# One tile for the attention's seven PSUM banks, handed out by a walk at build time

## The chip, the cores and the metric

The kernel runs on one core of a Trainium2 chip. Its engines work from queues of their own, in order, and wait for one another by semaphores: TensorE (PE) multiplies into PSUM, a memory of eight banks of 128 x 512 fp32; ScalarE (ACT) and VectorE (DVE) read PSUM; GpSimd (POOL) and the DMA queue of SyncE (SP) do not touch it here. The metric is the device time of one execution in microseconds, as the median of several.

## The reference

For x of 2048 tokens by 512 channels it computes a gated mix of attention and a token-mixing MLP:

```python
g = sigmoid((x * gate_w).sum(-1, keepdims=True))
qkv = (x @ wqkv).reshape(B, S, 3, H, Dh)            # S = 2048, H = 32 heads, Dh = 16
scores = einsum("bhqd,bhkd->bhqk", q, k) * Dh ** -0.5
a = einsum("bhqk,bhkd->bhqd", softmax(scores), v)   # then heads joined, @ wo
u = gelu(einsum("bsd,sf->bdf", layernorm(x), w1) + b1)     # F = 1792
b = einsum("bdf,fs->bds", u, w2) + b2               # back to (B, S, D)
return g * a + (1 - g) * b
```

All is fp32. With 32 heads of 2048 x 2048 scores, 134 million exponentials have to be taken, and an engine takes them 128 rows at a time.

## The kernel before, in words

The program has three stretches. Up to some 278 us it projects x to q, k and v (each fp32 product made of three products of split halves) and runs the first layer of the MLP. From 278 to 1231 us it runs the attention, with the second layer of the MLP woven in. A short end adds the last projection and stores the rows.

The attention has 32 groups (NG: 16 pairs of heads by two halves of the queries) of four phases each (PHASES), 128 phases in all, p = 0 to 127. A phase makes 16 score tiles (NSC), n = 0 to 15, each 128 keys by 512 queries, one matmul (line 1067) into one PSUM bank. A score uses 64 of PE's 128 rows; on the other 64 a product of the second layer, of a late projection or of the output projection runs beside it (line 1076, tile `dn`, which holds the eighth bank for itself). `dense` says how many products a phase has beside its scores: 14 in 96 phases, 12 in 32. The scores after that number have no product beside them; two of these that use different halves of the rows (`head`) run side by side.

Each score tile leaves PSUM in one of three ways:

- EVAC, n = 1, 3, 5, 8, 14, 15: DVE copies it to SBUF (line 1089, into `pe`), and one wide ACT instruction per phase takes the exponential of all six there (line 1102).
- SINGLE, n = 0, 2, 4, 6, 7, 9: ACT takes its exponential straight from PSUM (line 1093, 128 x 512).
- TWO, (10, 11) and (12, 13): two scores in neighbouring banks, one ACT instruction over both (line 1031, `exps`, 128 x 1024).

Then `apply_v` multiplies with v (line 963): 64 matmuls in groups of four that run side by side, adding into one bank, `av`. The pairs of scores are used in two lists: HELD (the copied ones, 3 pairs) are those of the phase before, since their wide exponential comes late; TURNS (5 pairs) are this phase's. DVE then adds `av` to a running sum in SBUF (line 985). In the first phase of a group (ph = 0) there are two such sums in two banks, one that ends the group before and one that begins the new group.

Seven banks serve 16 scores and one or two `av`. Before the change a phase opens two pools, one after the other (`regions`). The first has seven tiles of a bank each, for scores 0 to 6, and again for 7, 8 and 9. The second has two tiles of two banks for the pairs, two of one bank for scores 14 and 15, and `av`. `shares` decides which bank is which from the bank that `av` of the phase before had (`spare`), so that score n + 7 always takes the bank of score n, and `av` that of score 9. A score may be written when the tile that lay in its place has been read.

The order of the work on every engine is the order of the program's text (`manual_schedule`). In phases with 12 products beside, the text issues scores 12, 13, 15, 14 (`in_turn`), else 0 to 15 in order. Work of other kinds is hung between: `amid` before score 14's reader, `later` at the end of a phase on DVE, `calls` at its start. `mark` is a memset of one element on DVE that takes several waits at once so that later instructions wait for one engine alone; `evac_done` and `earlier` serve the same end.

Just ahead of the attention, line 549 on DVE reads the last two banks of layer 1 (`late_u`). Behind it, a pool `ps_end` opens seven tiles `pa` where the scores' banks lay; its first use sums the last `av` (lines 1169 and 1170).

Of the kernel before, what the change touches and what calls it, by code (L numbers as in the profile page):

```python
# [9 lines left out]
F32 = mybir.dt.float32  # L10
# [22 lines left out]
NB = 512  # L33
NQ = S // NB
VC = DH + 1
SCALE = DH**-0.5
# [24 lines left out]
def gated_mix(ctx: ExitStack, tc: tile.TileContext, a_x, a_wqkv, a_wo, b_w1, b_b1, b_w2, b_b2, gate_w, out):  # L61
    nc = tc.nc
# [115 lines left out]
    with tc.tile_pool(name="vp", bufs=1, side="right") as pool:  # L178
# [138 lines left out]
        e = pool.tile([P, NS], F32, name="e")  # L317
# [4 lines left out]
        y, t, w = (pool.tile([P, NS], F32, name=n) for n in "ytw")  # L322
# [103 lines left out]
    with tc.tile_pool(name="gl", bufs=2, side="right") as gl:  # L426
# [74 lines left out]
        for f0, cs in order.items():  # L501
            n = min(NB, F - f0) // P
# [32 lines left out]
    ptp = att_ctx.enter_context(tc.tile_pool(name="pt", bufs=2, reuse_waits="tile"))  # L535
# [45 lines left out]
    PHASES, NSC, BANKS = 4, 16, 7  # L581
    LAST = NG * PHASES - 1
# [257 lines left out]
    dense = {}  # L840
# [74 lines left out]

    token, mark = (out_pool.tile([1, 1], F32, name=name, bufs=1) for name in ("token", "mark"))

    EVAC = 1, 3, 5, 8, 14, 15
    SINGLE = 0, 2, 4, 6, 7, 9
    TWO = (10, 11), (12, 13)  # L920
    TURNS = [(0, 2), (4, 6), (7, 9), *TWO]
    HELD = [(1, 3), (5, 8), (14, 15)]

    def shares(n):

        for one in range(0, BANKS, 2):
            lows = [k for k in range(one)][::2] + [k for k in range(one + 1, BANKS)][::2]
            for third in lows:
                if n in (third, third + 1):
                    first, second = (low for low in lows if low != third)  # L930
                    return [first, first + 1, one, second, second + 1, 2 * third + 1 - n, n]


    def regions():
        return tc.tile_pool(name="ps_s", bufs=1, space=PSUM, reuse_waits="tile")

    sums, latest, evac_done = {}, {}, []

# [49 lines left out]

    engines = {getattr(mybir.EngineType, name) for name in ("PE", "Activation", "DVE", "Pool", "SP")}
    with tc.manual_schedule(engines=engines):  # L990
        held, fence, turn, spare = [], None, 0, 0
        landed.clear()

        for p in range(LAST + 1):
# [18 lines left out]
            if n_b == NSC - 2:  # L1013
                head[-2:] = second, 1 - second
            else:
                head[-4:] = second, 1 - second, 1 - second, second
            in_turn = list(range(n_b)) + ([14, 15] if n_b == NSC - 2 else [12, 13, 15, 14])
            qbs = {}
            for a, b in TURNS + HELD:
                if head[a] == head[b]:  # L1020
# [3 lines left out]
                    qbs[zero], qbs[one] = turn, 1 - turn  # L1024
                    turn = 1 - turn

            def exps(n):
                pt = ptp.tile([P, 2, NB], F32, name="p2", bufs=len(TWO))
                where = [share[(j - BANKS) % BANKS] for j in (n - 1, n)]
                low = min(where)  # L1030
                pairs_done.append(nc.scalar.activation(pt, twos[low, low + 1], AF.Exp, scale=SCALE))  # L1031
                for j, k in zip((n - 1, n), where):
                    units[j] = *units[j][:3], pt[:, k - low, :]

            pairs_done = []
            evac = evp.tile([P, len(EVAC), NB], F32, name="pe")
            units = {}
            share = shares(spare)
            pool = regions()
            psum = pool.__enter__()  # L1040
            ones = [psum.tile([P, NB], F32, name=f"s{n}") for n in range(BANKS)]
            for n in in_turn:
                i, qb = head[n], qbs[n]
                c = at[i][qb]
                at[i][qb] += 1
                if n < TWO[0][0]:
                    if n >= BANKS:
                        ones[share[n - BANKS]] = psum.tile([P, NB], F32, name=f"s{share[n - BANKS]}")
                    s = ones[share[n % BANKS]]
                else:  # L1050
                    if n == TWO[0][0]:
                        pool.__exit__(None, None, None)
                        pool = regions()
                        psum = pool.__enter__()
                        twos = {}
                        for low in range(BANKS):
                            if low == share[2]:
                                av = psum.tile([P, NB], F32, name="av")
                            elif low in (share[0], share[1]):
                                twos[low] = psum.tile([P, NB], F32, name=f"u{low}")  # L1060
                            elif low not in twos:
                                two = psum.tile([P, 2, NB], F32, name=f"t{low}")
                                twos[low], twos[low + 1] = two[:, 0, :], two[:, 1, :]
                                twos[low, low + 1] = two
                    s = twos[share[(n - BANKS) % BANKS]]
                rows_i = slice(i * HALF, i * HALF + ROWS)
                nc.tensor.matmul(  # L1067
                    s,
                    kt[grp][rows_i, c * P : (c + 1) * P],
                    qt[grp][rows_i, qb * NB : (qb + 1) * NB],  # L1070
                    start=True,
                    stop=True,
                )
# [8 lines left out]
                if n == in_turn[-2]:  # L1082
                    if n_b and second and beside[-1][-1] in between:
                        between[beside[-1][-1]]()
                    for what, *args in amid.get(p, ()):
                        what(*args)
                if n in EVAC:
                    pt = evac[:, EVAC.index(n), :]
                    nc.vector.tensor_copy(pt, s)  # L1089
                    units[n] = i, c, qb, pt  # L1090
                elif n in SINGLE:
                    pt = ptp.tile([P, NB], F32, name="p1", bufs=len(SINGLE))
                    one = nc.scalar.activation(pt, s, AF.Exp, scale=SCALE)  # L1093
                    if n == SINGLE[-1] and p:
                        tc.add_manual_dep(one.ins, earlier.ins.name, SYNC, reason=EARLY)
                    units[n] = i, c, qb, pt
                else:
                    units[n] = i, c, qb, None
                    if n in (TWO[0][1], TWO[1][1]):
                        exps(n)  # L1100
            for x in ([evac] if p < LAST else [evac[:, :2, :], evac[:, 2:, :]]):
                done = nc.scalar.activation(x, x, AF.Exp, scale=SCALE)  # L1102
# [19 lines left out]
            spare = share[2]  # L1122
# [19 lines left out]
            pool.__exit__(None, None, None)  # L1142
# [168 lines left out]
```

## Time and profile before

| | |
|---|---|
| median of 3 runs | 1265.29 us (1265.22 to 1266.12) |
| the profiled execution: span, first to last instruction | 1263.6 us |
| mean granted clock of PE in it | 0.998 |
| PE busy | 1255.3 us, 99% |
| ACT busy | 1069.0 us, 85% |
| DVE busy | 851.3 us, 67% |
| ACT busy between 500 and 700 us | 200.00 us |
| scores (line 1067), instructions | 2048 |
| exponentials from PSUM, single and pairs | 768 and 256 |

No time of its own was taken of the profiled execution but the span, which is 1.7 us below the median of the runs. How to read it: a row of the timeline is start, duration (us), engine, line, operation, tiles written <- tiles read, shapes, how many were merged, and in brackets the idle time before it with the one who ended it. PE's weight loads have a row of their own (PEld); a matmul that has to wait, waits in its weight load. A row whose instruction starts before the one ahead has ended means that the engine took it into its queue; its duration then holds waiting too. The span of a run of instructions in the timeline is from the first's start to the last's end.

### The profile page before, as it was taken

How to read it: one execution, taken by the hardware profiler on the slowest of the kernel's cores; microseconds unless marked ns; L12 is line 12 of the kernel's file. 1: busy time of each engine (PE TensorE's matmuls, PEld its weight loads, DVE VectorE, ACT ScalarE, POOL GpSimd, SP SyncE). 2: the span in 40 equal slices, each digit the busy share in tenths (PEclk: the TensorE clock that was granted, in tenths of full speed). 3: DMA queues.
4: the chain of work that ended last, by engine and by line, in shares of the span. 5: the costliest groups of instructions: out<-in, count | busy, mean ns of one | idle time of the engine just before them, and what ended most of it. 6: DMA issues, size and time to landing. Idle time of an engine off the chain costs nothing.

```text
span 1263.6 us, 32707 instructions
## 1 busy us (share of the span) xinstructions
PE 1255.3 (99%) x13342; PEld 828.5 (66%) x13342; DVE 851.3 (67%) x1562; ACT 1069.0 (85%) x1405; POOL 198.9 (16%) x316
## 2 busy tenths in 40 slices
PE   9999999999999999999999999999999999999997
PEld 7888888875666666666666666666666666666666
DVE  5675453178767676767677677776777677678883
ACT  4443343269999999999999999999999999999990
POOL 0220444461010101010101101111111111000000
PEclk9999999999999999999999999999999999999999
DMA  4799443243744444544344443443543442366611
GB/s 132 252 333 334 145 120 105 83 129 108 214 122 104 89 102 85 157 86 97 77 105 93 97 93 84 91 88 79 114 102 71 91 100 60 56 164 177 152 59 70
DMA packets 100555, 152.31 MB, mean 121 GB/s; under 512 B 17109, under 2 KB 56171, under 8 KB 96300
## 3 DMA queue, kind: packets, MB, share of 16 engines
q1 hardware_dynamic: 99820, 149.08, 45.9%
q8 instruction: 107, 1.75, 0.6%
q10 hardware_dynamic: 576, 1.05, 0.2%
q14 instruction: 52, 0.43, 0.1%
HBM read 105.39 MB, written 44.68 MB: 119 GB/s over the span
## 4 chain that ended last, share of the span: by engine, by line
PE 99%; ACT 1%; DVE 0%; issue 0%
PE av L963 31%; PE s L1067 22%; PE acc L424 12%; PE t L1067 9%; PE acc L75 8%; PE t L963 5%; PE dn L1076 4%; PE u L1067 3%; PE pa L1162 2%; PE acc L199 1%; PE acc L268 1%; PE acc L245 0%; ACT p L1093 0%; ACT pe L1102 0%; PE dn L1162 0%; PE pa L1192 0%
## 5 line engine op out<-in xcount | busy, mean ns | idle before, releaser
L1093 ACT ACTIVATE p<-s 128x512 f32<-128x512 f32 x768 | 412.4, 791 | 0.1
L1102 ACT ACTIVATE pe<-pe 128x3072 f32<-128x3072 f32 x129 | 381.7, 2961 | 0.0
L1067 PE MATMUL s<-qs,ks 64*128 64x512 f32 x1280 | 330.2, 400 | 0.6 <-ACT p L1093 0.6
L1089 DVE COPY pe<-s 128x512 f32<-128x512 f32 x512 | 318.2, 683 | 4.8 <-PE s L1067 1.1
L1067 PEld LDWEIGHTS s<-qs,ks 64*128 64x128 f32 x1280 | 225.6, 184 | 93.3 <-issue 45.3
L1031 ACT ACTIVATE p<-t 128x1024 f32<-128x1024 f32 x256 | 278.5, 1265 | 0.0
L963 PE MATMUL av<-p,v 128*32 128x256 f32 x3880 | 227.1, 379 | 0.0
L1089 DVE COPY pe<-u 128x512 f32<-128x512 f32 x256 | 164.9, 686 | 72.0 <-PE u L1067 72.0
L963 PE MATMUL av<-pe,v 128*32 128x256 f32 x3072 | 192.5, 383 | 0.0
L985 DVE TENSOR_TENSOR ot<-av,ot 128x512 f32<-128x512 f32 (+2 forms) x160 | 93.2, 583 | 142.3 <-PE av L963 141.0
L68 POOL TENSOR_TENSOR w_lo<-w_raw,w_hi 128x512 fp32r<-128x512 f32 (+1 forms) x128 | 153.1, 1203 | 197.3 <-ACT w_hi L67 100.3
L1076 PE MATMUL dn<-u_hi,w_hi 64*128 64x512 f32 x448 | 181.1, 404 | 0.0
L963 PEld LDWEIGHTS av<-p,v 128*32 128x32 f32 x3880 | 126.0, 110 | 83.3 <-ACT p L1093 0.2
L1076 PE MATMUL dn<-u_hi,w_lo 64*128 64x512 f32 x448 | 180.6, 403 | 0.0
L1076 PE MATMUL dn<-u_lo,w_hi 64*128 64x512 f32 x448 | 180.4, 403 | 0.0
L1067 PE MATMUL t<-qs,ks 64*128 64x512 f32 x512 | 142.2, 412 | 0.0
L963 PEld LDWEIGHTS av<-pe,v 128*32 128x32 f32 x3072 | 86.7, 109 | 82.1 <-ACT p L1093 37.8
L1080 POOL MEMSET token<- 1x1 f32 x128 | 11.4, 89 | 742.2 <-PE dn L1076 701.7
L67 ACT CAST w_hi<-w_raw 128x512 fp32r<-128x512 f32 (+1 forms) x67 | 38.0, 569 | 82.9 <-PE acc L424 63.1
L1067 PEld LDWEIGHTS t<-qs,ks 64*128 64x128 f32 x512 | 72.9, 184 | 51.0 <-ACT p L1093 49.5
L424 PE MATMUL acc<-h_hi,w_hi 128*128 128x512 f32 x224 | 87.9, 392 | 0.0
L424 PE MATMUL acc<-h_hi,w_lo 128*128 128x512 f32 x224 | 87.8, 392 | 0.0
(171 smaller groups left out, 1616.0 us busy)
## 6 DMA issues: line engine op xcount, KB each, us to landing
w_raw<-in_B_w_dram SPq DMA_DIRECT2D x96, 256.0 KB
ks<-kp SPq DMA_DIRECT2D x192, 128.0 KB
qs<-qp SPq DMA_DIRECT2D x256, 64.0 KB
kp<-pc SPq DMA_DIRECT2D x16, 512.0 KB
qp<-pc SPq DMA_DIRECT2D x8, 768.0 KB
qp<-row SPq DMA_DIRECT2D x24, 256.0 KB
v<-v SPq DMA_DIRECT2D x4, 1088.0 KB
x<-in_A_x_dram SPq DMA_DIRECT2D x16, 256.0 KB
```

The costliest lines, as they stand in the source:

```text
L67: copy(hi, src)
L68: return sub(lo, src, hi.bitcast(F32), ALU.subtract)
L75: nc.tensor.matmul(ps, a, b, start=start and n == 0, stop=stop and n == last)
L424: nc.tensor.matmul(p, a, b, start=first and k == 0, stop=last and k == 2)
L963: mm = nc.tensor.matmul(av[32 * j : 32 * (j + 1), i * QC : (i + 1) * QC], vb[b][:, v_at : v_at + 32], pt[:, h * QC : (h + 1) * QC], start= ...
L985: latest["add"] = nc.vector.tensor_tensor(x, y, x, ALU.add)
L1031: pairs_done.append(nc.scalar.activation(pt, twos[low, low + 1], AF.Exp, scale=SCALE))
L1067: nc.tensor.matmul(s, kt[grp][rows_i, c * P : (c + 1) * P], qt[grp][rows_i, qb * NB : (qb + 1) * NB], start=True, stop=True,)
L1076: mm = nc.tensor.matmul(ps, a[half], b[half], start=begin and not second, stop=last and bool(second))
L1089: nc.vector.tensor_copy(pt, s)
L1093: one = nc.scalar.activation(pt, s, AF.Exp, scale=SCALE)
L1102: done = nc.scalar.activation(x, x, AF.Exp, scale=SCALE)
```

## The change

The seven banks become one tile that lives through the whole attention, and each score's bank is a slice of it. Which slice is settled at build time by a new function, `given_out`. It walks through the 128 phases with times that are written in it as constants (a score every 0.2305 us, a single exponential every 0.488 us, a pair 0.914, a copy 0.6 and so on), keeps for each bank when it will be free, and gives each score the bank that is free first; a pair gets the two neighbouring banks of which the later is free first; `av` gets the bank that is free first too. It returns, for each phase, the banks of the 16 scores and of the one or two `av`. `shares`, `regions` and the pools of each phase go. EVAC, SINGLE, TWO, TURNS and HELD are now worked out from a string, KINDS, and all scores are issued in the order 0 to 15.

```diff
-    EVAC = 1, 3, 5, 8, 14, 15
-    SINGLE = 0, 2, 4, 6, 7, 9
-    TWO = (10, 11), (12, 13)
-    TURNS = [(0, 2), (4, 6), (7, 9), *TWO]
-    HELD = [(1, 3), (5, 8), (14, 15)]
-    def shares(n):
...
-    def regions():
-        return tc.tile_pool(name="ps_s", bufs=1, space=PSUM, reuse_waits="tile")
+    KINDS = "sesesessesaabbee"
+    SINGLES = 6
...
+    def given_out():
+        free, vector, scalar, stream, load, wide = [0.0] * BANKS, 0.0, 0.0, 0.0, 0.0, 0.0
+        given = []
+        def first_free(spread=1, at=None):
+            ways = [b for b in range(BANKS + 1 - spread)] if at is None else [at]
+            best = min(ways, key=lambda b: (max(free[b : b + spread]), b))
+            when = max(free[best : best + spread])
+            free[best : best + spread] = [1e9] * spread
+            return best, when
+        for p in range(LAST + 1):
+            singles = len(dense.get(p // 2, ()))
+            bank, open_two, scored, readers = {}, {}, {}, {}
+            copied = []
+            for n, kind in enumerate(KINDS):
+                alone = n < singles or (n - singles) % 2 == 0
+                if kind in "es":
+                    bank[n], when = first_free()
+                elif kind not in open_two:
+                    bank[n], when = first_free(2)
+                    open_two[kind] = bank[n] + 1, when
+                else:
+                    bank[n], when = open_two[kind]
+                start = max(when + 0.05, stream, load) if alone else max(when + 0.05, begun)
+                load = 0.0
+                begun, stream = start, start + 0.2305
+                scored[n] = start + 0.44
+                if kind == "e":
+                    vector = max(vector + 0.6, scored[n] + 0.69)
+                    free[bank[n]] = vector
+                    copied.append(vector)
+                elif kind == "s":
+                    scalar = max(scalar + 0.488, scored[n] + 0.6)
+                    free[bank[n]] = readers[n] = scalar
+                elif kind in readers:
+                    scalar = max(scalar + 0.914, scored[n] + 1.02)
+                    free[bank[n] - 1 : bank[n] + 1] = [scalar] * 2
+                    readers[n] = scalar
+                else:
+                    readers[kind] = None
+            done = sorted([x for x in readers.values() if x] + [readers[two[1]] for two in TWO])
+            scalar = max(scalar, max(copied) + 0.25) + 0.4267 * len(EVAC) + 0.093
+            sums = [first_free()]
...
+            vector = max(vector + 1.6, at + 1.0)
+            free[sums[-1][0]] = vector
+            load = at + 0.3
+            given.append(([bank[n] for n in range(NSC)], [b for b, _ in sums]))
+        return given
...
-        held, fence, turn, spare = [], None, 0, 0
+        held, fence, turn = [], None, 0
+        given = given_out()
+        scores_ctx = ExitStack()
+        ps_s = scores_ctx.enter_context(tc.tile_pool(name="ps_s", bufs=1, space=PSUM, reuse_waits="tile"))
+        banks = ps_s.tile([P, BANKS, NB], F32, name="banks")
...
-            head = [second if n < n_b else (second + NSC - 1 - n) % 2 for n in range(NSC)]
...
-            in_turn = list(range(n_b)) + ([14, 15] if n_b == NSC - 2 else [12, 13, 15, 14])
+            head = [second if n < n_b else (second + n - n_b) % 2 for n in range(NSC)]
...
+            bank, av_banks = given[p]
...
+                pairs_done.append(nc.scalar.activation(pt, banks[:, low : low + 2], AF.Exp, scale=SCALE))
...
-            share = shares(spare)
-            pool = regions()
-            psum = pool.__enter__()
-            ones = [psum.tile([P, NB], F32, name=f"s{n}") for n in range(BANKS)]
-            for n in in_turn:
+            av = banks[:, av_banks[0]]
+            for n in range(NSC):
...
-                    s = twos[share[(n - BANKS) % BANKS]]
+                s = banks[:, bank[n]]
...
-            tc.add_manual_dep(done.ins, pairs_done[0].ins.name, SYNC, reason=EARLY)
+            tc.add_manual_dep(done.ins, pairs_done[-2].ins.name, SYNC, reason=EARLY)
             evac_done.append(done)
-            earlier = pairs_done[1]
+            earlier = pairs_done[-1]
...
-                    spare = share[3]
-                    av = twos[spare]
+                    av = banks[:, av_banks[1]]
...
-            pool.__exit__(None, None, None)
...
+        scores_ctx.close()
```

More of the change, by code (lines that the diff above doesn't have):

```diff
@@ L916, in gated_mix @@
     token, mark = (out_pool.tile([1, 1], F32, name=name, bufs=1) for name in ("token", "mark"))
-    EVAC = 1, 3, 5, 8, 14, 15
-    SINGLE = 0, 2, 4, 6, 7, 9
-    TWO = (10, 11), (12, 13)
-    TURNS = [(0, 2), (4, 6), (7, 9), *TWO]
-    HELD = [(1, 3), (5, 8), (14, 15)]
-    def shares(n):
[L926 to L931, printed above, removed]
@@ L934, in regions @@
-    def regions():
-        return tc.tile_pool(name="ps_s", bufs=1, space=PSUM, reuse_waits="tile")
+    KINDS = "sesesessesaabbee"
+    SINGLES = 6
+    EVAC = [n for n, kind in enumerate(KINDS) if kind == "e"]
+    SINGLE = [n for n, kind in enumerate(KINDS) if kind == "s"]
+    TWO = [tuple(n for n, kind in enumerate(KINDS) if kind == two) for two in sorted(set(KINDS) - {"e", "s"})]
+    assert all(len(two) == 2 for two in TWO) and len(KINDS) == NSC
+    own = sorted([(n, n) for n in SINGLE] + [(two[1], n) for two in TWO for n in two])
@@ new lines, in gated_mix @@
+    own = [n for _, n in own]
+    kept = list(EVAC)
+    if len(own) % 2:
+        own.remove(SINGLE[-1])
+        kept.append(SINGLE[-1])
+    TURNS, HELD = ([(x[i], x[i + 1]) for i in range(0, len(x), 2)] for x in (own, kept))
+    def given_out():
[40 more added lines that the diff above has]
+            sums = [first_free()]
+            at = max(stream + 0.12, sums[0][1])
+            at += 0.2157 * 2 * len(HELD)
+            if p % PHASES == 0 and p:
+                free[sums[0][0]] = at + 1.1
+                sums.append(first_free())
+                at = max(at, sums[1][1])
+            for i in range(0, 2 * (len(done) // 2), 2):
+                at = max(at, done[i + 1] + 0.05) + 0.2157 * 2
+            vector = max(vector + 1.6, at + 1.0)
[3 more added lines that the diff above has]
+        return given
@@ L1025, in gated_mix, with exps @@
                     turn = 1 - turn
-            def exps(n):
+            bank, av_banks = given[p]
+            def exps(two):
                 pt = ptp.tile([P, 2, NB], F32, name="p2", bufs=len(TWO))
[L1029 to L1033, printed above, removed]
+                low = bank[two[0]]
+                assert bank[two[1]] == low + 1
+                pairs_done.append(nc.scalar.activation(pt, banks[:, low : low + 2], AF.Exp, scale=SCALE))
+                for k, j in enumerate(two):
+                    units[j] = *units[j][:3], pt[:, k, :]
             pairs_done = []
@@ L1045, in gated_mix @@
                 at[i][qb] += 1
[L1046 to L1051, printed above, removed]
-                        pool.__exit__(None, None, None)
[L1053 to L1064, printed above, removed]
-                    s = twos[share[(n - BANKS) % BANKS]]
+                s = banks[:, bank[n]]
                 rows_i = slice(i * HALF, i * HALF + ROWS)
@@ L1081, in gated_mix @@
                         tc.add_manual_dep(fence.ins, mm.ins.name, SYNC, reason=REASON)
-                if n == in_turn[-2]:
+                if n == NSC - 2:
                     if n_b and second and beside[-1][-1] in between:
@@ L1091, in gated_mix @@
                 elif n in SINGLE:
-                    pt = ptp.tile([P, NB], F32, name="p1", bufs=len(SINGLE))
+                    pt = ptp.tile([P, NB], F32, name="p1", bufs=SINGLES)
                     one = nc.scalar.activation(pt, s, AF.Exp, scale=SCALE)
@@ L1098, in gated_mix @@
                     units[n] = i, c, qb, None
-                    if n in (TWO[0][1], TWO[1][1]):
-                        exps(n)
+                    for two in TWO:
+                        if n == two[1]:
+                            exps(two)
             for x in ([evac] if p < LAST else [evac[:, :2, :], evac[:, 2:, :]]):
                 done = nc.scalar.activation(x, x, AF.Exp, scale=SCALE)
-            tc.add_manual_dep(done.ins, pairs_done[0].ins.name, SYNC, reason=EARLY)
+            tc.add_manual_dep(done.ins, pairs_done[-2].ins.name, SYNC, reason=EARLY)
             evac_done.append(done)
-            earlier = pairs_done[1]
+            earlier = pairs_done[-1]
             if n_b and second and beside[-1][-1]:
@@ L1121, in gated_mix @@
             turns, now_held = ([tuple(units[n] for n in pair) for pair in pairs] for pairs in (TURNS, HELD))
-            spare = share[2]
             if ph == 0:
@@ L1141, in gated_mix @@
                 last_ot = ot
-            pool.__exit__(None, None, None)
             held = now_held
```

4 lines of the change are left out of this document (removed).

## The prediction, made before the result was known

> **What bounds the kernel now.** The page first: which engines are full, and where the chain of work runs.
>
> ```profile
> span 1263.6 us, 32707 instructions
> ...
> PE 1255.3 (99%) x13342; PEld 828.5 (66%) x13342; DVE 851.3 (67%) x1562; ACT 1069.0 (85%) x1405; POOL 198.9 (16%) x316
> ...
> PE 99%; ACT 1%; DVE 0%; issue 0%
> ```
>
> The chain lies on PE to 99%, but that alone does not make PE the limit: a busy PE may be one that is held back. So next the window of the attention, which is all that the change touches.
>
> ```profile
> core 0: us, PE busy (x) PEld busy (x) DVE busy (x) ACT busy (x) POOL busy (x), PEclk, DMA share, GB/s
> 286.00:1227.00 941.00, 940.37 (x11838) 577.00 (x11840) 685.22 (x1285) 941.00 (x1146) 98.88 (x220) 1.00 0.45 104
> ```
>
> Here ACT is busy for 941.00 of 941.00 us and PE for 940.37, at a granted clock of 1.00. Two engines are full, so the question is which one paces. The timeline of ACT around the middle shows one phase (16 score tiles), and the timeline of the same phase shows who waits.
>
> ```profile
> 699.47 3.00 ACT L1102 ACTIVATE pe<-pe 128x3072 f32<-128x3072 f32 x1
> ...
> 702.16 3.24 ACT L1093 ACTIVATE p<-s 128x512 f32<-128x512 f32 x6
> 705.05 2.19 ACT L1031 ACTIVATE p<-t 128x1024 f32<-128x1024 f32 x2
> 706.88 3.01 ACT L1102 ACTIVATE pe<-pe 128x3072 f32<-128x3072 f32 x1
> 709.58 0.80 ACT L1093 ACTIVATE p<-s 128x512 f32<-128x512 f32 x1
> ```
> ```profile
> 701.63 0.49 PE L1067 MATMUL s<-qs,ks 64*128 64x512 f32 x1
> ...
> 702.39 2.48 DVE L1089 COPY pe<-s 128x512 f32<-128x512 f32 x4
> 702.39 0.69 DVE L1089 COPY pe<-s 128x512 f32<-128x512 f32 x1
> ...
> 703.81 0.39 PE L1067 MATMUL s<-qs,ks 64*128 64x512 f32 x1
> ...
> 703.99 0.18 PEld L1067 LDWEIGHTS t<-qs,ks 64*128 64x128 f32 x1 [0.22 <-ACT p L1093]
> ...
> 704.03 0.46 PE L1067 MATMUL t<-qs,ks 64*128 64x512 f32 x1
> ...
> 704.48 0.18 PEld L1067 LDWEIGHTS t<-qs,ks 64*128 64x128 f32 x1 [0.19 <-ACT p L1093]
> ...
> 704.97 0.19 PEld L1067 LDWEIGHTS u<-qs,ks 64*128 64x128 f32 x2 [0.19 <-ACT p L1093]
> ...
> 705.46 1.02 PEld L963 LDWEIGHTS av<-pe,v 128*32 128x32 f32 x24 [0.30 <-ACT p L1093]
> 705.46 1.50 PE L963 MATMUL av<-pe,v 128*32 128x256 f32 x24
> ...
> 706.78 2.34 PE L963 MATMUL av<-p,v 128*32 128x256 f32 x40
> ...
> 709.05 0.18 PEld L1067 LDWEIGHTS s<-qs,ks 64*128 64x128 f32 x1 [0.41 <-issue]
> 709.05 0.50 PE L1067 MATMUL s<-qs,ks 64*128 64x512 f32 x1
> ```
>
> From the start of score 0 (call it T = 701.63) to the next one at 709.05 is 7.42 us. Within it PE waits for ACT four times in these rows: for a bank that an exp has still to read. That is the sign that ACT paces and PE follows. How closely it follows is told by a phase in which PE ran without such waits, and by three wide exps after a short starvation of ACT.
>
> ```profile
> 1124.73 0.50 PE L1067 MATMUL s<-qs,ks 64*128 64x512 f32 x1
> ...
> 1132.05 0.49 PE L1067 MATMUL s<-qs,ks 64*128 64x512 f32 x1
> ```
> ```profile
> 343.40 3.00 ACT L1102 ACTIVATE pe<-pe 128x3072 f32<-128x3072 f32 x1
> ...
> 348.98 2.19 ACT L1031 ACTIVATE p<-t 128x1024 f32<-128x1024 f32 x2
> 351.10 2.77 ACT L1102 ACTIVATE pe<-pe 128x3072 f32<-128x3072 f32 x1
> ...
> 358.44 2.83 ACT L1102 ACTIVATE pe<-pe 128x3072 f32<-128x3072 f32 x1
> ```
>
> PE alone needs 1132.05 - 1124.73 = 7.32 us a phase. ACT needs 7.42: the wide exps start 7.70 and 7.34 apart (343.40, 351.10, 358.44), but end, by start plus duration, at 346.40, 353.87 and 361.27, 7.47 and 7.40 apart. A start 0.28 late cost the end some 0.05. So ACT has a queue that hides lateness, and its ends keep 7.42 whatever its starts do. PE has only 7.42 - 7.32 = 0.10 us to spare in each of 128 phases. That is the number on which this prediction turns.
>
> How long is ACT's queue? An exp that starts behind a full queue takes 0.80 (the row at 709.58); the one behind the starved wide exp took 581 ns:
>
> ```profile
> L1093 ACT ACTIVATE p<-s 128x512 f32<-128x512 f32 x1 | 0.6, 581 | 0.0
> ```
>
> The difference, 0.22, is how late score 0 can come without ACT standing still. The wide exp gives a like number: it began 351.10 - 348.98 = 2.12 after the pairs where it usually begins 706.88 - 705.05 = 1.83 after them, 0.29 late, and lost 0.05, so 0.24. I take 0.20 as the lag of PE that ACT forgives, since both readings are upper ends for a phase in which both points are late; 0.15 and 0.30 are kept for the range.
>
> **The change part by part.** No matmul, exp, copy or transfer is added or removed; SP's and POOL's queues get the same instructions in the same order. KINDS spells the same six copied, six single and four paired scores, and TURNS and HELD come out as the same lists. The last wide exp is tied to pairs_done[-2] and the next phase to pairs_done[-1]; with two pairs these are the old [0] and [1]. In the 32 phases with 12 products beside, the issue order 12, 13, 15, 14 becomes 12, 13, 14, 15, but the halves of the rows still alternate, so the same two scores run side by side and two copies on DVE change places. All that costs 0.
>
> What changes is which bank a score gets, and so for which reader PE waits. Write e4 for the exp of score 4, c5 for the copy of score 5. Relative to T, a weight load that waited for e4 began at 703.99, 2.36; for e6 at 704.48, 2.85; for for e7 at 704.97, 3.34; for e9 (av) at 705.46, 3.83. Four copies take 2.48 from 702.39, the first alone 0.69, so they end 0.60 apart; with 0.05 to wake PE they free banks at 1.50 (c1), 2.09 (c3), 2.69 (c5) and 3.29 (c8). A score that waited ends 0.50 after its weight load; those that run freely end 0.23 apart; score 0 ends at 0.50. Score 14 would freely end at 0.50 + 14 x 0.23 = 3.73, and the next T follows 3.59 after it: 7.32, as measured. To keep ACT's 7.42, score 14 may end at 3.83.
>
> Old: every phase reuses banks in one order: scores 7 to 15 take those freed by e0 c1 e2 c3 e4 c5 e6 e7 c8, which is the order of their release (c8 and e7 aside, and those two scores run together). No other order can be quicker. Score 10 also waits for the second bank of its pair, e4, so it ends at 2.36 + 0.50 = 2.86 instead of 2.80; this wait goes with the shared tile, and is worth nothing, since score 11 needs e4 at the same time and ACT is full anyway.
>
> New: I followed given_out() line by line for its bank numbers alone (its times are not used). After the first four phases 27 different orders occur in 124 phases, because a pair needs two neighbouring banks and takes the pair whose later bank comes first. Phase 18, for one, gives scores 0 to 6 banks 3 4 5 6 1 2 0, 7 to 9 banks 3 4 5, the pairs 1 2 and 3 4, and 14, 15 banks 6 0. So score 12 waits for e7 and 13 for c8. It ends score 12 at 3.84, 13 at 4.07, 14 at 4.30, 0.47 over 3.83. If PE already lags ACT by 0.20, everything that ACT frees comes 0.20 earlier on PE's clock, what DVE frees does not: 12 at 3.64, 13 at 3.87, 14 at 4.10, 0.27 over. Since PE can lag by no more than 0.20 without starving ACT, that 0.27 is lost.
>
> The same sum for all 124 phases, carrying the lag from one phase to the next (a phase in the old order gives back 0.10 at most, 0.04 at a lag of 0.20, where c8 holds score 15), comes out thus; after each class what a phase is over at a lag of 0 and of 0.20:
> - 38 phases in the old order or one as good: 0.01 and -0.04; lost 0.05 in all
> - 13 with c3 and e6 for 12 and 13 (e6 then holds 13): 0.06 and 0.06; lost 0.2
> - 26 with e6 for score 10 or 11: 0.22 and 0.02; lost 0.4
> - 26 with e7 for 13: 0.24 and 0.04 to 0.06; lost 1.2
> - 5 with c8 for 13: 0.19 and 0.19; lost 0.7
> - 16 with e7 for 12, or e6 for 10 ahead of c5 and c3: up to 0.48 and 0.29; lost 3.8
>
> Sum 6.3 us. With 0.10, 0.15, 0.25, 0.30 and 0.50 for the forgiven lag the same sum gives 13.0, 9.6, 4.2, 3.4 and 1.8.
>
> Six phases of before already start their wide exp late, as at 351.10; the last is this:
>
> ```profile
> 1209.66 2.19 ACT L1031 ACTIVATE p<-t 128x1024 f32<-128x1024 f32 x2
> 1211.80 2.77 ACT L1102 ACTIVATE pe<-pe 128x3072 f32<-128x3072 f32 x1
> ```
>
> There DVE's extra work has used up the queue, so PE's lag of 0.20 is lost once in each: 6 x 0.2 = 1.2.
>
> **The start.** Here the two views are DVE against PE as layer 1 ends.
>
> ```profile
> 277.44 1.40 DVE L549 TENSOR_SCALAR row<-acc,b 128x512 f32<-128x512 f32 x2
> ...
> 277.77 0.50 PE L1067 MATMUL s<-qs,ks 64*128 64x512 f32 x1
> ...
> 278.23 0.18 PEld L1067 LDWEIGHTS s<-qs,ks 64*128 64x128 f32 x1 [0.28 <-DVE row L549]
> ...
> 278.30 1.30 ACT L1093 ACTIVATE p<-s 128x512 f32<-128x512 f32 x2
> ```
>
> L549 reads the last two banks of layer 1 until 277.44 + 1.40 = 278.84. The old first phase leaves late banks to late scores (banks 1 and 0 go to scores 5 and 6), and score 1 alone waits, for the first of the two reads. The new one gives score 0 bank 0, and one tile over seven banks is first written when all are free. So score 0 moves from 277.77 to 278.84 + 0.05 = 278.89. Old, the wait of score 1 left a hole in ACT: two exps take 1.30 from 278.30 where 0.58 + 0.48 would do (six take 705.05 - 702.16 = 2.89). That hole of 0.2 closes: 1.1 - 0.2 = 0.9, with 0 (waits per bank that find bank 0 free) and 1.1 as ends.
>
> **The end.** The end's seven tiles open where the one tile lay, and must await both last additions rather than one.
>
> ```profile
> 1231.02 0.76 DVE L985 TENSOR_TENSOR ot<-av,ot 128x256 f32<-128x256 f32 x2 [0.48 <-PE av L963]
> ...
> 1231.68 0.59 PE L1169 MATMUL pa<-ot,sums_of 128*128 128x256 f32 x2
> ```
>
> They end at 1231.02 + 0.76 = 1231.78; with 0.05 the matmul moves from 1231.68 to 1231.83, +0.1 (0 to 0.15). PE also leaves the attention with its lag of 0.2.
>
> **Sum.** 0.9 + 6.3 + 1.2 + 0.1 + 0.2 = 8.7 us. The profiled span is 1263.6, 1.7 under the median of 1265.29; span 1272.3, so 1274.0 in the runs' terms.
>
> **Rivals.**
> (a) No measurable change, the other side: ACT forgives far more than 0.20. The place is the wide exp, 2.7 us of work in one instruction; decided at a lag of about 0.5, where the sum is 1.8 and the six phases cost nothing. 1265.3 + 0.9 + 1.8 = 1268, or 1266 to 1267 if the start is free as well. Against it: 0.29 already cost 0.05.
> (b) Faster: 7.42 is not ACT's but a loop over PE (e9 frees av, av ends, score 0, exp 0; exp 0 starts 0.03 after 709.05 + 0.50), and a freer PE brings 7.32: 127 x 0.10 = 12.7, so 1253. Against it: ends 7.40 apart where starts were 7.34.
> (c) A bigger loss: ACT forgives 0.10 to 0.15 only, as DVE's copies of 14 and 15 shift with PE. 9.6 to 13.0 and 2.4 beside: 1277 to 1281.
> (d) The guard is on the tile, not the bank, and scores wait for readers of other banks. A score every 0.50 + 0.48 instead of 0.23 adds some 0.75 x 16 x 128 = 1500 us. The code before had pair tiles of two banks whose waits were for both, which is a small case of it. The Trainium skill, "PSUM — Partial Sum Buffer", section "PSUM bank collisions raise a hardware error", asks that PSUM be guarded by bank and quadrant, by bank in the simple version, not by address: by that rule a bank is enough and (d) is not needed; no run here shows it yet.
> (e) The clock: PE's more frequent short waits lower the granted clock. At half speed a phase of PE takes 7.32 more; in one phase of twenty that is 6 x 7.32 = 44 us, 1318. The row at 286.00 has 1.00 although PE waits up to 0.41 at a time. The Trainium skill, "TensorE: Matmul & The Clock Gate", section "A second HAM failure mode: psum-queue depth-cycling", tells of a kernel whose short idles between groups of matmuls, from cycling through PSUM banks, made the clock swing between half and full; the trace so far does not agree.
>
> **How the numbers follow.** Forecast 0.64, with its own range 1270 to 1279 (lags 0.15 to 0.30, start 0 to 1.1); (a) 0.12, (b) 0.04, (c) 0.16, (d) 0.02, (e) 0.02. About 0.2%, 2.5 us, is what can be told from no change here. Slower is the forecast, (c), (d) and (e): 0.84; same (a): 0.12; faster (b): 0.04. The range reaches into (a), to 1266, and over (c), to 1286; it leaves out (b), (d), (e) and an edge of (a) and (c).
>
> **What would show it.** Right: idle of ACT before L1093 or L1102 in the window 286 to 1227, some 6 to 8 us in all where there was none; phases of 7.42 mixed with some of 7.6 to 7.8; weight loads of scores 11 to 13 waiting for ACT or DVE by 0.2 to 0.5; score 0 at 278.9. Wrong: wide exps ending 7.42 apart throughout, or score 0 at 277.8.

## The result: three times the time

The changed kernel takes 3986.49 us (3982.20 to 3987.83, 4 runs) against 1265.36 us (1265.22 to 1266.12) for the kernel before on the same chip: a ratio of 3.150 [3.146, 3.155]. The forecast was 1274.0. The profiled span is 3983.9 us. The page of the changed kernel, the lines that answer to those of before (PEclk is the granted clock of PE in 40 slices of the span, in tenths):

```profile
span 3983.9 us, 32292 instructions
...
PE 2437.3 (61%) x13342; PEld 1088.5 (27%) x13342; DVE 906.6 (23%) x1562; ACT 1193.0 (30%) x1405; POOL 197.8 (5%) x316
...
PEclk9996565656656565666656556665555655556667
...
PE 63%; ACT 18%; DVE 16%; issue 3%; DVEq 0%
...
L1099 PE MATMUL banks<-qs,ks 64*128 64x512 f32 x2048 | 1393.2, 714 | 1408.1 <-ACT p L1125 524.4
L1099 PEld LDWEIGHTS banks<-qs,ks 64*128 64x128 f32 x2048 | 515.7, 269 | 2288.3 <-ACT p L1125 870.2
...
L1016 PE MATMUL banks<-p,v 128*32 128x256 f32 x5120 | 402.4, 474 | 32.0 <-DVE ot L1038 31.2
L1016 PE MATMUL banks<-pe,v 128*32 128x256 f32 x3072 | 355.6, 632 | 99.5 <-DVE mark L1144 50.9
```

The counts of instructions are those of before (PE 13342, ACT 1405, DVE 1562). No engine is full any more, and the chain runs through all three in turn. That is how work looks that is handed from one engine to the next, one piece at a time. The timeline shows the hand:

```profile
2000.22 0.60 ACT L1125 ACTIVATE p<-banks 128x512 f32<-128x512 f32 x1 [2.46 <-PE dn L1108]
...
2000.87 0.79 PE L1099 MATMUL banks<-qs,ks 64*128 64x512 f32 x1 [0.68 <-ACT p L1125]
...
2001.69 0.60 ACT L1125 ACTIVATE p<-banks 128x512 f32<-128x512 f32 x1 [0.88 <-PE dn L1108]
...
2002.35 0.79 PE L1099 MATMUL banks<-qs,ks 64*128 64x512 f32 x1 [0.69 <-ACT p L1125]
...
2003.17 0.69 DVE L1121 COPY pe<-banks 128x512 f32<-128x512 f32 x1 [3.84 <-PE dn L1108]
...
2003.92 0.79 PE L1099 MATMUL banks<-qs,ks 64*128 64x512 f32 x1 [0.78 <-DVE pe L1121]
```

One score, its reader, the next score: 1.48 us a step after an exp, 1.57 after a copy, where before the scores went 0.23 apart. With seven banks to write to, each score waits until the score just ahead of it has been read. The view of waits counts it:

```profile
PEld banks L1099 <- ACT p L1125: 870.2, 768, 1.2
PEld banks L1099 <- DVE pe L1121: 789.6, 640, 1.3
...
PEld banks L1099 <- ACT p L1085: 462.4, 256, 1.8
...
PEld banks L1099 <- DVE ot L1038: 164.7, 127, 1.5
```

The columns are us in total, times, longest. 768 + 640 + 256 + 127 = 1791 waits, which is 14 in each of 128 phases, less the first: behind every single exp, five of six copies, every pair, and the addition of `av`. Only the second score of each pair does not wait. The four sum to 2286.9 of the 2288.3 us that the scores' weight loads stood idle.

The books close on PE. Before, a phase was 3.83 us of scores (701.63 to 705.46) and 3.59 of multiplying with v (705.46 to 709.05): 490 and 460 us over 128 phases. After, the scores have 1393.2 us of matmuls and 1408.1 of idle ahead of them, the products with v 402.4 + 355.6 and 32.0 + 99.5. That is 3690.8 - 950 = 2741 us more, against 3983.9 - 1263.6 = 2720 in the spans. The 950 are one phase times 128, so the last 21 us are not accounted for.

### The profile page after: what moved, and what is told of

Read it like the earlier page. It is cut to its first block, busy times and chain, and to the rows that moved or that the text cites. A ratio compares the mean times of both kernels' runs of the same rounds, so it can differ in the third digit from the quotient of the medians.

```text
span 3983.9 us, 32292 instructions
## 1 busy us (share of the span) xinstructions
PE 2437.3 (61%) x13342; PEld 1088.5 (27%) x13342; DVE 906.6 (23%) x1562; ACT 1193.0 (30%) x1405; POOL 197.8 (5%) x316
## 4 chain that ended last, share of the span: by engine, by line
PE 63%; ACT 18%; DVE 16%; issue 3%; DVEq 0%
PE banks L1099 35%; PE banks L1016 19%; DVE pe L1121 13%; ACT p L1125 12%; ACT p L1085 7%; PE acc L424 4%; PE acc L75 3%; DVE ot L1038 2%; PE dn L1108 1%; PE pa L1193 1%; PE acc L199 0%; PE acc L268 0%; DVEq L1038 0%; PE acc L245 0%; DVE mark L1144 0%
## 5 line engine op out<-in xcount | busy, mean ns | idle before, releaser
L1099 PE MATMUL banks<-qs,ks 64*128 64x512 f32 x2048 | 1393.2, 714 | 1408.1 <-ACT p L1125 524.4
L1099 PEld LDWEIGHTS banks<-qs,ks 64*128 64x128 f32 x2048 | 515.7, 269 | 2288.3 <-ACT p L1125 870.2
L1121 DVE COPY pe<-banks 128x512 f32<-128x512 f32 x768 | 531.1, 692 | 2245.2 <-PE dn L1108 1263.0
L1125 ACT ACTIVATE p<-banks 128x512 f32<-128x512 f32 x768 | 458.6, 597 | 1856.2 <-PE dn L1108 1331.3
L1016 PE MATMUL banks<-p,v 128*32 128x256 f32 x5120 | 402.4, 474 | 32.0 <-DVE ot L1038 31.2
L1016 PE MATMUL banks<-pe,v 128*32 128x256 f32 x3072 | 355.6, 632 | 99.5 <-DVE mark L1144 50.9
L1085 ACT ACTIVATE p<-banks 128x1024 f32<-128x1024 f32 x256 | 262.1, 1024 | 321.7 <-PE banks L1099 175.1
L1108 PE MATMUL dn<-u_lo,w_hi 64*128 64x512 f32 x448 | 316.5, 706 | 0.0
L1108 PE MATMUL dn<-u_hi,w_hi 64*128 64x512 f32 x448 | 313.6, 700 | 0.0
L1016 PEld LDWEIGHTS banks<-p,v 128*32 128x32 f32 x5120 | 198.0, 141 | 259.3 <-issue 143.2
L424 PE MATMUL acc<-h_hi,w_hi 128*128 128x512 f32 x224 | 87.9, 392 | 0.0
L424 PE MATMUL acc<-h_hi,w_lo 128*128 128x512 f32 x224 | 87.8, 392 | 0.0
```

What stands on the lines that cost most here:

```text
L424: nc.tensor.matmul(p, a, b, start=first and k == 0, stop=last and k == 2)
L1016: mm = nc.tensor.matmul(av[32 * j : 32 * (j + 1), i * QC : (i + 1) * QC], vb[b][:, v_at : v_at + 32], pt[:, h * QC : (h + 1) * QC], start= ...
L1085: pairs_done.append(nc.scalar.activation(pt, banks[:, low : low + 2], AF.Exp, scale=SCALE))
L1099: nc.tensor.matmul(s, kt[grp][rows_i, c * P : (c + 1) * P], qt[grp][rows_i, qb * NB : (qb + 1) * NB], start=True, stop=True,)
```

## The experiments

Four theories were set against each other. **G**: the program's guard, the waits that keep a bank from being written before it is read, follows the tile, whatever bank a score takes. **W**: the walk's order of banks costs the time. **K**: the clock does. **O**, which came up on the way: the order costs more than the prediction's sum. Kernel 4, say, is the kernel of experiment 4.

**1. The old order in the one tile.** given_out() returns the numbers that `shares` gave; all else is as changed.

```diff
     def given_out():
+        def shares(n):
...
         for p in range(LAST + 1):
+            share = shares(spare)
+            bank = [share[n % BANKS] for n in range(NSC)]
+            bank[12:14] = sorted(bank[12:14])
+            sums = [share[2]] + ([share[3]] if p and p % PHASES == 0 else [])
+            spare = sums[-1]
```

> The changed kernel with the bank numbers of the kernel before (score n + 7 takes the bank of score n), in the one tile. Theory G (the waits are set per tile, so that a score waits for the reader of the score before it, in whatever bank): as slow as the changed kernel, 3900 to 4050 us. Rival W (the order in which the walk hands out banks is what costs): back near 1265 us. Rival K (the clock falls of itself because of short waits of PE, and the order brings those waits): near 1265 us too, at a granted clock near 1.00.

Measured in one run: 3984.49 us, as the changed kernel. W and K expected some 1265. So the walk's order is not what costs the 2720 us; the loss comes with the one tile.

**2. The walk's order in the old pools.** The kernel before, with the bank numbers and the order of issue of the change.

```diff
+            bank, av_banks = given[p]
...
-            share = shares(spare)
...
-                    s = twos[share[(n - BANKS) % BANKS]]
+                    s = twos[bank[n]]
```

> The kernel before with its two pools per phase and its separate tiles, but with the bank numbers and the issue order of the walk. Theory G: about the blind forecast, since only the order is left: 1274 us, 1268 to 1280, at a granted clock near 1.00; PE waits 0.2 to 0.5 us ahead of scores 11 to 13 in many phases. Rival W: near 3986 us. If PE's lag is forgiven by ACT to any depth: 1266 us.

Measured: 1303.44 us (1303.12 to 1303.71), ratio 1.0300 [1.0286, 1.0314]. W's 3986 is out, but G's own figure of 1274 is missed too: the order costs 38 us in these pools where the prediction's sum gave 9. That opened O, to which experiments 8 and 9 return.

**3 and 4. PE's waits by bank, in the one tile.** Each score, and the first product of each `av`, waits for the last readers of its own bank alone, with the walk's order (3) and the old one (4). The readers' own waits are left as they were.

```diff
+    def wrote(mm, b, *source):
+        mine = readers.get(b, [])
...
+        tc.declare_no_dep(mm.ins, group="bank readers", keep=keep, reason="other banks")
+        for x in mine:
+            tc.add_manual_dep(mm.ins, x.ins.name, SYNC, reason="this bank was read")
...
+                wrote(sc, bank[n])
```

> The changed kernel (one tile, banks by the walk), but each score and each sum told to wait for the readers of its own bank alone: the waits for other banks are taken off, those for the own bank stated by hand. Theory G: 1274 us as for the walk in old pools, at most 2 us off, since the work and the banks are the same and the pair's first score no longer waits for the second bank. Rival W: near 3986 us.

> One tile with the bank numbers of the kernel before, and waits per bank. Theory G: 1265 to 1267 us, the kernel before but for the start (up to 1.1 us, if the first score waits for all seven banks). Rival that a tile of seven banks costs something of itself (long patterns, other semaphores): above 1270.

Measured: 2011.53 us, ratio 1.590 [1.588, 1.592], and 2017.20, 1.594 [1.592, 1.596]. Half a cure, which no theory had foreseen: G's figures are missed by some 740 and 750 us. The waits and the timeline of kernel 4 name the rest:

```profile
DVE pe L1113 <- ACT p L1117: 440.6, 507, 2.6
ACT p L1117 <- DVE pe L1113: 361.6, 441, 1.1
DVE pe L1113 <- ACT p L1072: 319.4, 128, 2.8
```
```profile
1009.73 0.60 ACT L1117 ACTIVATE p<-banks 128x512 f32<-128x512 f32 x1 [0.82 <-DVE pe L1113]
1010.36 0.69 DVE L1113 COPY pe<-banks 128x512 f32<-128x512 f32 x1 [0.72 <-ACT p L1117]
...
1011.15 0.60 ACT L1117 ACTIVATE p<-banks 128x512 f32<-128x512 f32 x1 [0.82 <-DVE pe L1113]
```

ACT and DVE take turns: an exp waits for the copy of another bank, the copy for the exp. Exp to exp is 1.42 us: 0.60 + 0.69, and 0.13 for two wake-ups. So the guard on the tile also sets its two readers one behind the other. Why it does so, when both only read, no run here shows.

**5 and 6. All waits by bank, in the one tile.** As 3 and 4, and ACT's and DVE's readers no longer wait for each other.

```diff
+    def has_read(inst, *of, own="ACT"):
+        tc.declare_no_dep(inst.ins, group="DVE" if own == "ACT" else "ACT", reason="other banks")
+        tc.add_to_no_dep_group(own, inst.ins)
...
+                    has_read(one, bank[n])
```

> One tile, banks by the walk, with waits per bank for PE and now also none left between a copy on DVE and an exp on ACT of different banks (the run with PE's waits alone set per bank stayed at 2011 us, and its trace showed the readers waiting for each other). Theory G, with the order's cost as the blind sum has it: 1274 us, 1268 to 1280. Rival O (the order alone costs more than the sum, as the 1303 us of the walk in old pools say): 1285 to 1303. If the guard has yet another part: far above 1303.

> One tile, bank numbers of the kernel before, waits per bank for all three engines. Theory G: 1265 to 1267 us, since then nothing is left of the change but the first score's wait for all seven banks (0.9 us). Rival that a tile of seven banks costs something of itself: above 1270.

Measured: walk 1269.27 us (1269.11 to 1269.86), ratio 1.0031 [1.0019, 1.0042]; old order 1265.55 (1265.06 to 1266.12), 1.0002 [0.9993, 1.0011]. Both lie in G's ranges. With the waits by bank the one tile costs nothing that the time shows, and the walk some 4 us. The other 2717 us (3986.49 - 1269.27) go with the waits for banks that an instruction does not touch; the fall of the clock (experiment 7), which goes with them too, is in that sum.

Where the 4 us lie is told by the last matmul of layer 1 (L424) and the first and the 127th wide exp, in the kernel before, in 5 and in 6:

```profile
277.45 0.39 PE L424 MATMUL acc<-h_hi,w_lo 128*128 128x512 f32 x1
...
283.21 2.83 ACT L1102 ACTIVATE pe<-pe 128x3072 f32<-128x3072 f32 x1
...
1219.14 2.83 ACT L1102 ACTIVATE pe<-pe 128x3072 f32<-128x3072 f32 x1
```
```profile
277.26 0.39 PE L424 MATMUL acc<-h_hi,w_lo 128*128 128x512 f32 x1
...
283.92 2.84 ACT L1173 ACTIVATE pe<-pe 128x3072 f32<-128x3072 f32 x1
...
1223.15 2.77 ACT L1173 ACTIVATE pe<-pe 128x3072 f32<-128x3072 f32 x1
```
```profile
277.01 0.39 PE L424 MATMUL acc<-h_hi,w_lo 128*128 128x512 f32 x1
...
283.67 2.84 ACT L1134 ACTIVATE pe<-pe 128x3072 f32<-128x3072 f32 x1
...
1219.42 2.85 ACT L1134 ACTIVATE pe<-pe 128x3072 f32<-128x3072 f32 x1
```

By start plus duration the ends of the wide exps are 935.93 apart before, 939.16 in 5 and 935.76 in 6. The walk costs 3.2 us in 126 phases. Layer 1 ends a few tenths apart in the three traces, so the start is counted from its last matmul: the first wide exp ends 8.59 us after it starts before, and 9.50 in 5 and in 6. The start costs 0.91 in both, though the time of 6 does not show it.

**7. The clock alone.** In the changed kernel the tile has six banks, and on the seventh PE repeats each score's matmul three times, so that its pauses are filled. The result uses none of these.

```diff
-    PHASES, NSC, BANKS = 4, 16, 7
+    PHASES, NSC, BANKS = 4, 16, 6
...
+        fill = ps_s.tile([P, NB], F32, name="fill")
...
+                for _ in range(3):
+                    nc.tensor.matmul(
+                        fill,
...
```

> The changed kernel with six banks in the tile instead of seven, and the seventh used for three idle copies of each score's matmul, issued behind the score and waited for by nobody, so that PE works through its pauses. The outputs are the same. Theory that the low granted clock (0.60 in the attention) is an effect of PE's pauses and adds to the loss: the clock goes back to 0.95 or more, a score that waited takes 0.50 instead of 0.79, and the time falls from 3986 to 2900 to 3200 us, although 6144 matmuls are added. Rival that the clock has fallen for another reason: the clock stays, and the time rises.

Measured in one run: 3603.4 us. A window of the attention in the changed kernel, then in this one; the number behind the five engines' busy times (and their instructions) is the granted clock:

```profile
300.00:3900.00 3600.00, 2092.05 (x11740) 827.72 (x11740) 732.55 (x1270) 1054.28 (x1130) 97.96 (x219) 0.60 0.11 27
```
```profile
300.00:3500.00 3200.00, 2916.94 (x17628) 1652.40 (x17617) 726.33 (x1260) 1047.38 (x1126) 98.39 (x217) 0.93 0.13 30
```
And the scores on this kernel's timeline:

```profile
1505.89 0.50 PE L1100 MATMUL banks<-qs,ks 64*128 64x512 f32 x1 [0.82 <-DVE ot L1038]
...
1507.07 0.49 PE L1100 MATMUL banks<-qs,ks 64*128 64x512 f32 x1
...
1508.35 0.50 PE L1100 MATMUL banks<-qs,ks 64*128 64x512 f32 x1
```

With the pauses between scores filled the clock is 0.93 instead of 0.60 (0.95 or more was expected), a score takes 0.50 instead of 0.79, and a step 1.18 after an exp and 1.28 after a copy. The kernel gains 383 us, less than the 800 to 1100 expected. That is a net figure: the added matmuls take time of their own, and 20% of the chain that ended last lies on them on this kernel's page. So the clock follows the pauses, and some seventh of the loss is the least that it costs; its full share is not measured.

**8 and 9. What the walk costs in the old pools.** Kernel 5, in which the first score of a pair waits for the readers of both banks, as a tile of two banks makes it (8); and in which also the second `av` of a group's first phase keeps the other bank of the pair's tile, of which it is a slice (9; the line with `shared` is in 9 alone).

```diff
-                wrote(sc, bank[n])
+                pair_of = [bank[n] + 1] if n in (TWO[0][0], TWO[1][0]) else []
+                pair_of += shared.pop(bank[n], [])
+                wrote(sc, bank[n], beside=pair_of)
```

> The walk's order with waits per bank (1269.3 us), but the first score of each pair, 10 and 12, waits for the last readers of both banks of its pair, as the tiles of two banks made it do. The walk hands out two neighbours at the time when the later of them is read, so the walk allows for this, and theory O (order costs more than the sum when tiles span two banks) splits in two. O1: the pairs' waits delay ACT a little in every phase; the kernel with the old pools had wide exps 7.6 us apart in most phases against 7.44, 0.16 x 127 = 20 us, so 1289 (1280 to 1297). O2: the pairs' waits are hidden, since scores 11 and 13 wait a moment later anyway, and only the second av costs: 1269 to 1272.

> The kernel with pair waits, and in the 31 phases that begin a group after the first the second av, a slice of a tile of two banks with the old pools, also keeps that tile's other bank: the next phase's score on it waits for DVE's add of that av. Theory O says that these two waits are the whole of what the old pools cost under the walk's order: 1303 (1298 to 1308), of which the av is 31 x about 0.5 = 16 us. Rival: the old pools cost by something else as well (a score that waits for TensorE's own earlier write of a bank, a new pool in mid-phase): then this stays below 1298.

Measured: 1286.19 us (1285.98 to 1286.64), ratio 1.0166 [1.0151, 1.0182], and 1301.32 (1300.96 to 1301.48), 1.0285 [1.0269, 1.0301]. Both lie in the ranges of O (O1 for the pairs). From 1269.27, the pairs cost 16.9 and the second `av` 15.1; 2.1 are left to the 1303.44 of kernel 2, and stay open. The weight loads of scores 0 and 12 and of the first product with v, and the wide exps, of kernel 8, then a line of the waits of kernel 9:

```profile
651.57 0.18 PEld L1132 LDWEIGHTS banks<-qs,ks 64*128 64x128 f32 x1 [0.41 <-issue]
...
654.72 0.18 PEld L1132 LDWEIGHTS banks<-qs,ks 64*128 64x128 f32 x1 [0.54 <-ACT p L1161]
...
655.62 1.02 PEld L1035 LDWEIGHTS banks<-pe,v 128*32 128x32 f32 x24 [0.36 <-issue]
```
```profile
649.47 2.77 ACT L1174 ACTIVATE pe<-pe 128x3072 f32<-128x3072 f32 x1
657.10 2.77 ACT L1174 ACTIVATE pe<-pe 128x3072 f32<-128x3072 f32 x1
664.72 2.77 ACT L1174 ACTIVATE pe<-pe 128x3072 f32<-128x3072 f32 x1
```
```profile
PEld banks L1132 <- DVE ot L1065: 25.9, 25, 1.2
```

The phase's score 0 is the row at 651.57, so score 12 comes 3.15 after it, after the phase's only wait for a bank. The products with v begin 4.05 after score 0 instead of 3.83 before; with their 3.59 that is 7.64, and the wide exps are 7.63 and 7.62 apart instead of 7.42. This is the common case: of the 126 distances between the ends of wide exps, 84 are over 7.55 in kernel 8, 15 in kernel 5 and 2 in the kernel before. In kernel 9 a score waits 25 times for DVE's addition, 1.0 us each; the waits of kernels 5 and 8 in the attention have no such line.

**10. Less work for ACT.** With waits by bank, three pairs in place of two pairs and two of the singles.

```diff
-    KINDS = "sesesessesaabbee"
-    SINGLES = 6
+    KINDS = "seseseseaabbccee"
+    SINGLES = 4
```

> The walk with waits per bank, and the kinds changed: three pairs of scores for two singles less (seseseseaabbccee; four singles, six copies, three pairs), so that ACT has less to do: two singles at 0.488 against one pair at 0.914 save it 0.06 us a phase, 8 us over 127. If ACT still paces, 1261 to 1264, which is under both kernels; if the walk loses the gain again because three pairs, two late copies and the av want nine of seven banks, 1267 to 1285.

Measured: 1313.80 us (1313.40 to 1314.25), ratio 1.0384 [1.0370, 1.0398]: a miss beyond both guesses. A window of the attention, and the waits:

```profile
286.00:1270.00 984.00, 978.33 (x11782) 598.02 (x11778) 681.97 (x1277) 957.64 (x1011) 99.43 (x220) 1.00 0.44 99
```
```profile
PEld banks L1132 <- DVE pe L1156: 38.5, 113, 0.7
...
PEld banks L1132 <- ACT p L1160: 29.7, 102, 0.8
PEld banks L1132 <- ACT p L1115: 26.2, 104, 0.8
```

ACT is busy for 957.64 of 984.00 us and does not pace any more; by these lines the scores' weight loads wait 94.4 us for banks in 319 places. In kernel 5 they wait 51.0 in 171:

```profile
PEld banks L1132 <- ACT p L1160: 38.4, 123, 1.0
...
PEld banks L1132 <- DVE pe L1156: 12.6, 48, 0.6
```

That fits the second guess, a shortage of banks, but does not show it. The 43 us between the two are near the 44.5 between the kernels, yet such a sum is no measure of a loss: before the change the same waits make 79.2 us in 373 places, and the kernel is quicker. No run here changes the number of pairs alone, without the order in which the kinds follow. No kernel here beats the one before.

## Why the prediction was wrong

The forecast gave the right sign and missed the size by 2712 us. What happened is rival (d), with (e) in its train, at a chance of 0.02 each.

The step that failed is the one under "New": score 12 "waits for e7 and 13 for c8", that is, for the reader of its own bank, inside a tile of seven. Two sentences of the prediction's own text spoke against it. "The start" has one tile that "is first written when all are free", a wait by tile; and (d) names the pair tiles whose waits were for both banks. The sum counted a wait by tile where the tile begins, and by bank everywhere else. The ground on which (d) was put aside was the Trainium skill, "PSUM — Partial Sum Buffer", section "PSUM bank collisions raise a hardware error". Its rule agrees with kernels 5 and 6: waits by bank are enough, and cost 1269.27 and 1265.55 us. But it tells what has to be guarded, and the question was what this program guards. The trace of before showed it only in the pairs' tiles of two banks, where it cost nothing.

The price of (d), 1500 us, was too low as well. It counted 0.98 a step, 0.50 for the score and 0.48 for its reader; the steps took 1.48 and 1.57, because a score took 0.79 as the clock fell, and an exp that starts alone 0.60, a copy 0.69, with some 0.1 for the wake-ups; and it left out that the products with v slow down too (758.0 us against 460).

(e) put the fall of the clock at one phase in twenty. The mean in the window is 0.60, and PEclk reads 5 or 6 in every slice from the fourth to the last but one, so it falls all through the attention. The Trainium skill, "TensorE: Matmul & The Clock Gate", section "A second HAM failure mode: psum-queue depth-cycling", tells of a swing between half and full from short idles, and here the trace agrees. In windows of 4 us from 1000 to 1060 of the changed kernel the granted clock is 0.50 in nine of fifteen and 1.00 in two, and each of the two comes right behind a window in which PE was busy for at least 3.97 us, with products with v.

The parts of the sum can be judged by kernel 5, which does what the prediction took the change to do. It took 1269.27, some 4 us over before, where 8.7 was forecast:
- Start: 0.9 forecast, 0.91 measured. Right, and score 0 did start when L549 was through (277.57 + 0.73 = 278.30), as the changed kernel's timeline has it. It comes 1.44 us after the start of the last matmul of layer 1 (276.92), where before it came 0.32 after it: 1.12 later, as forecast.

```profile
277.57 0.73 DVE L549 TENSOR_SCALAR row<-acc,b 128x512 f32<-128x512 f32 x1
...
278.36 0.50 PE L1099 MATMUL banks<-qs,ks 64*128 64x512 f32 x1 [1.05 <-DVE row L549]
```

- Order of banks: 6.3, and 1.2 for the late phases, forecast; 3.2 for both measured. The mechanism was right in kind: 13 more phases than before are longer than 7.55 us (7.56 to 7.93). It was mis-sized: ACT stood idle for 1.57 of the 941 us from 286 to 1227, where 6 to 8 were to show it. The lag that ACT forgives may be the reason: the prediction's table with its late phases gives 3.4 + 6 x 0.3 = 5.2 at a lag of 0.30, and 1.8 at 0.50, so 3.2 lies between. That was not tested.
- Score 10's wait for its pair "is worth nothing": right for the old order (kernel 6, without it, equals before). In the walk's order the waits for both banks of a pair, of scores 10 and 12 together, cost 16.9 us.
- End and PE's last lag: 0.3 forecast. Not seen: from the end of the first wide exp to the end of the span kernel 5 takes 2.9 us more than before (980.44 against 977.56), no more than the 3.2 of its phases.

## What to carry to other kernels

Ask of every tile that many instructions share which part of it the program guards; here the tile of seven banks was one resource, and its writers and its readers queued behind one another as if there were one bank. Before a change that merges buffers is priced, look for a case of it in the kernel at hand (here the pairs' tiles of two banks), and let the trace and not a rule of the hardware say what is waited for. When every engine's share falls and the chain runs through all of them, count the waits by kind: here 14 in a phase named the cause.

## What was not expected of the hardware

- Pauses far shorter than a phase were enough to lower the clock for a whole stage: PE idle 0.68 to 0.78 us between scores, busy 2092 of 3600 us, granted clock 0.60; three more matmuls in each pause, busy 2917 of 3200 us, brought 0.93.
- ACT and DVE read different banks of PSUM side by side, and neither took longer for it. The first exp and the first copy of kernel 5 overlap, and take the 0.60 and 0.69 us that they take one at a time in the changed kernel. The turns that they took in kernels 3 and 4 were the program's.

```profile
279.23 0.60 ACT L1160 ACTIVATE p<-banks 128x512 f32<-128x512 f32 x1 [1.11 <-PE banks L1132]
...
279.46 0.69 DVE L1156 COPY pe<-banks 128x512 f32<-128x512 f32 x1 [0.81 <-PE banks L1132]
```

- A small wait counts where an engine has next to nothing to spare. PE had 0.10 us in a phase of 7.42; one wait of 0.54 ahead of score 12 went with a phase of 7.62, and the pairs' waits cost 16.9 us over the kernel.
